# A fused attention, gating and convolution kernel: two more additions in the last head pair, and the last two tiles of w_in loaded and converted through both buffers

## The chip, the cores and the metric

The kernel runs on one core of one Trainium2 chip, in one launch. The metric is the device time of that core in microseconds (us); 553.07 us is the median of three runs of the kernel before (552.95 to 553.29).

## The reference, cut to what matters

Three blocks follow one another. Inputs are float32; batch is 4, the sequence 576 long, 8 heads of 64, model width 512.

```python
# 1. attention, per batch and head, rotary q and k
attn = softmax(scale * q_rot @ k_rot.T); x = attn @ v          # -> [4, 576, 512]
# 2. gated MLP ("the MLP" below)
h = gelu_tanh(x @ w_in); u, v = h[..., :512], h[..., 512:]     # w_in is 512 x 1024
v_n = (v - mean(v)) / sqrt(var(v) + 1e-6) * g_ln
gated = u * (w_sg @ v_n + b_sg); x = x + gated @ w_out
# 3. convolution gate
gate = sigmoid(conv5(x)); out = (gate * (x @ w_val)) @ w_out2
```

## The kernel before, in words

**Attention.** The 32 heads are worked as 16 pairs (`NPAIR`, i = 0 to 15), two heads in the two halves of the 128 partitions. For a pair, `st_unit` makes transposed scores in nine units: keys in four chunks of 128, each in two halves of 288 queries (u = 0 to 7, table `UNITS`), and a unit u = 8 for the remaining 64 keys. ScalarE (ACT) takes the exponential of each unit into a tile `E`. `pv_unit` multiplies with v on TensorE (PE, L686 and L696), and `sum_unit` (L708) forms the softmax denominators, also on PE, by multiplying with ones in full float32 (L720): four matmuls per term, one for each head and query half. To have fewer terms, `add_unit` (L666) first adds units on GpSimd (POOL, the additions at L260) into two tiles `AC`, one per query half. `adds(i)` (L663) says how many additions a pair makes: 4 in pairs 9 to 14, so that chunks 0, 1 and 2 lie in `AC`; 2 in the others, pair 15 among them, where chunk 2 stays a term of its own in `sum_unit`. While pair i runs, VectorE (DVE) finds the row maxima of pair i + 1 (`s_unit`), so pair 15 has no such work beside it.

**w_in.** Weights arrive as raw 64-bit numbers. w_in is cut into eight tiles n = 0 to 7 (rows k = n % 4; tiles 0 to 3 hold columns 512 to 1023 and are used first, tiles 4 to 7 hold columns 0 to 511). For a tile, `wa_load` moves 512 KB by a DMA on SyncE's queue (SP) into a buffer `WR`; `wa_abs` takes the absolute value on ACT (L319) into `WT`; `wa_half`, twice, turns half a tile into float32 by four DVE instructions (L309, L311, L313, L315) into `WF`; `wa_split` copies the high part to `w_h` on ACT (L263) and subtracts it on POOL for the low part `w_l` (L260). There are two sets of the buffers: number 0 lives until the MLP's end, number 1 belongs to attention's memory and is given up with it. `place(n)` (L331) says which a tile uses: even and odd by turns up to tile 5, then buffer 0 for tiles 6 and 7. Tiles 4 and 5 are converted after pair 14, beside the preparation of the MLP's first input (`x_mult`, `x_high`, `x_low` for four head pairs), and tile 6 is loaded then (`job_v`, L435). Tiles 6 and 7 are converted in the MLP's part of the program (L1120 to L1122): tile 7's load waits until tile 6 has left buffer 0.

**The MLP's start.** `part_a(0)` runs three units of x times columns 512 to 1023 (tiles 0 to 3), each followed by a Gelu into a tile `gl` (L894), statistics, a scaling and a split into `vn` or, for the third unit, `t4` (shown as t); then four units `u_unit` with columns 0 to 511 (tiles 4 to 7, in the order of k); then four `g_unit` with `vn` and `t4`. The results `XH`, `XL` of the preparation are read by the first units.

**Memory and order.** The closing of attention's memory (`close_att`, L1095) is a task that depends on every task of attention, and what writes the MLP's tiles depends on it. By the sizes in the order of the code, the first `gl` tile lies at bytes 97,280 to 101,376 from the right edge; attention's `rc` (denominators) lies at 99,920 to 99,992 and its buffer `WR` number 1 at 99,992 to 104,088, so both are under it. A planner (`Plan`) takes tasks with a cost, their dependencies and a due time worked back from the end, and writes out one order per engine. PE keeps the order of the program; the other engines' queues and SP's are sorted by readiness and due time. Tasks marked `lock` on DVE and POOL are planned so as not to run at the same time. After attention there are the MLP for the three other batches, and the last block.

Of the kernel before, what the change touches and what calls it, by code (L numbers as in the profile page):

```python
# [22 lines left out]
NPAIR = B * HP  # L23
FOUR = 9
# [3 lines left out]
class Plan:  # L28
# [6 lines left out]
    def add(self, eng, cost, fn, r=(), w=(), after=(), lat=0.0, lock=False, kb=0.0):  # L35
        k = len(self.tasks)
        deps = set(after)
        for key in r:
            deps.update(self.writer.get(key, ()))
        for key in w:  # L40
            deps.update(self.writer.get(key, ()))
            deps.update(self.readers.get(key, ()))
        for key in r:
            self.readers.setdefault(key, []).append(k)
        for key in w:
            self.writer[key] = [k]
            self.readers[key] = []
        if eng == "PE":
            if self.last_pe is not None:
                deps.add(self.last_pe)  # L50
            self.last_pe = k
        deps.discard(k)
        self.tasks.append((eng, cost, fn, tuple(sorted(deps)), lat, lock, (tuple(w) or tuple(r))[0:1]))
        self.kb.append(kb)
        return k
# [87 lines left out]
def dve(n):  # L143
    return 0.08 + n / 960


def dve2(n):
    return 0.08 + n / 1920


def act(n):
    return 0.11 + 0.833e-3 * n
# [18 lines left out]
def mixer_kernel(ctx: ExitStack, tc: tile.TileContext, qk, v, vrem, cs, w_in, g_ln, w_sgT, b_sg,  # L171
# [4 lines left out]
    P = Plan()  # L176
# [11 lines left out]
    def tiles(pool_, name, n, shape, dt):  # L188
        T[name] = [pool_.tile(shape, dt, name=f"{name}{j}") for j in range(n)]
        return T[name]  # L190
# [23 lines left out]
    w_h = pA.tile([128, 4, 1024], F32R, name="w_h")  # L214
    w_l = pA.tile([128, 4, 1024], F32R, name="w_l")
# [4 lines left out]
    WR = tiles(pA, "wr", 1, [128, 512, 2], I32)  # L220
    WF = tiles(pA, "wf", 1, [128, 512], F32)
    WT = tiles(pA, "wt", 1, [128, 512], F32)
# [33 lines left out]
    def tt(e, out_, a, b, op, n, r, w, after=()):  # L256

        if e == "D":
            return add("DVE", dve(n), lambda: nc.vector.tensor_tensor(out_(), a(), b(), op), r, w, after, lock=True)  # L259
        return add("Pool", pool(n), lambda: nc.gpsimd.tensor_tensor(out_(), a(), b(), op), r, w, after, lock=True)  # L260

    def acopy(out_, in_, n, r, w, after=()):
        return add("Act", act(n), lambda: nc.scalar.copy(out_(), in_()), r, w, after)  # L263

    def pool_waits(src, r):

        return [add("Pool", 0.1, lambda: nc.gpsimd.tensor_copy(mark[0:1], src()), r, [("mark",)])]

    def split(hi, lo, src, n, rk, kh, kl, e="P", after=()):

        acopy(hi, src, n, rk, [kh], after)
        tt(e, lo, src, lambda: hi().bitcast(F32), ALU.subtract, n, [*rk, kh], [kl])
# [26 lines left out]
    def f64_to_32(raw, f, t, keys, n, after=()):  # L299


        kr, kf, kt = keys

        def i32(x):
            return x().bitcast(I32)

        def top():
            return raw()[:, :, 1]
        return [add("DVE", dve2(n), lambda: nc.vector.tensor_scalar(t(), t(), MIN_NORMAL, None, ALU.max), [kt], [(*kt, n, "x")],  # L309
                    after, lock=True),  # L310
                add("DVE", dve2(n), lambda: nc.vector.tensor_scalar(  # L311
                    i32(t), i32(t), 3, 0x3FFFFFF8, ALU.logical_shift_left, ALU.bitwise_and), w=[(*kt, n, "x")], lock=True),
                add("DVE", dve(n), lambda: nc.vector.scalar_tensor_tensor(  # L313
                    i32(t), raw()[:, :, 0], 29, i32(t), ALU.logical_shift_right, ALU.bitwise_or), [kr], [(*kt, n, "x")], lock=True),
                add("DVE", dve(n), lambda: nc.vector.scalar_tensor_tensor(  # L315
                    i32(f), top(), -0x40000000, i32(t), ALU.bitwise_and, ALU.bitwise_or), [kr, (*kt, n, "x")], [kt, kf], lock=True)][-1]

    def f64_abs(raw, t, keys, n, after=()):
        add("Act", act(n), lambda: nc.scalar.activation(t(), raw()[:, :, 1].bitcast(F32), AF.Abs), [keys[0]], [keys[2]], after)  # L319

    def weight_load(y, src, after=()):
        dma(512, lambda q: q.dma_start(out=WR[y].rearrange("p a b -> p (a b)"), in_=src), w=[("wr", y)], after=after)
# [6 lines left out]
        split(dst_h, dst_l, lambda: WF[0], 512, [("wf", 0)], (name, "h"), (name, "l"))  # L329

    def place(n):  # L331
        return n % 2 if n < 6 else 0

    def wa_load(n, after):
        k, hf = n % 4, 1 - n // 4
        weight_load(place(n), w_in[128 * k:128 * k + 128, 1024 * hf:1024 * hf + 1024], after)

    def wa_abs(n, after):
        y = place(n)
        f64_abs(lambda: WR[y], lambda: WT[y], [(m, y) for m in ("wr", "wf", "wt")], 512, after)  # L340

    def wa_half(n, x, after):
        y, cc = place(n), slice(256 * x, 256 * x + 256)
        k = f64_to_32(lambda: WR[y][:, cc], lambda: WF[y][:, cc], lambda: WT[y][:, cc], [(m, y) for m in ("wr", "wf", "wt")], 256, after)
        return [k]

    def wa_split(n, after):
        y, k, hf = place(n), n % 4, 1 - n // 4
        cc = slice(512 * hf, 512 * hf + 512)
        split(lambda: w_h[:, k, cc], lambda: w_l[:, k, cc], lambda: WF[y], 512, [("wf", y)], (f"win{k}_{hf}", "h"), (f"win{k}_{hf}", "l"),  # L350
              after=after)

    def sg_load(k, after):
# [24 lines left out]
    def wa_whole(n, after):  # L378
        wa_abs(n, after)
        for x in range(2):  # L380
            wa_half(n, x, after)
        wa_split(n, after)
# [35 lines left out]
    def job_v(i, after, rot):  # L418

        last = []  # L420
        if i % 2 and i < 8:
            wa_abs(i // 2, after)
        if not i:
            last = pool_waits(lambda: RAW[0][0:1, 1, 0, S - 1:S], [("raw", 0, 1)])
        if 1 <= i < 9:
            y, x = (i - 1) // 2 % 2, (i - 1) % 2
            wa_half((i - 1) // 2, x, rot)
            last = pool_waits(lambda: WF[y][0:1, 256 * x + 255:256 * x + 256], [("wf", y)])
        if i == 9 and FOUR > 9:
            last = pool_waits(lambda: RAW[1][0:1, 1, 0, S - 1:S], [("raw", 1, 1)])  # L430
        if FOUR <= i < NPAIR - 1:
            j3 = (i + 1) % 3
            low_part("D", i + 1, 1, rot)
            last = pool_waits(lambda: KL[j3].bitcast(F32)[0:1, S - 1:S], [("kl", j3)])
        if i == NPAIR - 2:  # L435
            for hp in range(2):
                x_mult(0, hp, after, "D")
                x_high(0, hp, after)
                x_low(0, hp, after)
                x_load(0, hp + 2, after)  # L440
            for n in (4, 5):
                wa_whole(n, after)
            wa_load(6, P.writer["xs", 1])
            for hp in (2, 3):
                x_mult(0, hp, after, "D")
                x_high(0, hp, after)
                x_low(0, hp, after)
        return last


# [110 lines left out]
    def low_part(e, i, j, after):  # L561

        j2, j3 = i % 2, i % 3
        hi, lo, kh, kl = ((QH, QL, "qh", "ql"), (KH, KL, "kh", "kl"))[j]
        tt(e, lambda: lo[j3], lambda: RAW[j2][:, j, 0], lambda: hi[j3].bitcast(F32), ALU.subtract, S,
           [("raw", j2, j), (kh, j3)], [(kl, j3)], after)
        if j:
            dma(32, lambda q: dg(q, KRL[j3], KL[j3]), [("kl", j3)], [("krl", j3)], n=2)
# [92 lines left out]
        EU[i, u] = n  # L661
        add("Act", 0.62, lambda: nc.scalar.activation(E[n], ps[:, :, 0:HALF], AF.Exp), [kps], [("e", n)])  # L662
    def adds(i):  # L663
        return 4 if FOUR <= i < NPAIR - 1 else 2

    def add_unit(i, u):  # L666

# [173 lines left out]
    def x_mult(b, hp, after=(), e="P"):  # L841
        i, y = 4 * b + hp, hp % 2
        tt(e, lambda: XS[y][:, 4:], lambda: XS[y][:, 4:], lambda: RB[y][:, 4:], ALU.mult, S, [("rb", y)], [("xs", y)], after)
        dma(290, lambda q: q.dma_start(out=x_d[i], in_=XS[y][:, 4:]), [("xs", y)], [("x_d", i)])

    def x_high(b, hp, after=()):
        add("Act", act(S), lambda: nc.scalar.copy(XH[:, hp], XS[hp % 2][:, 4:]), [("xs", hp % 2)], [("X", hp, "h")], after)

    def x_low(b, hp, after=()):
        return [tt("D", lambda: XL[:, hp], lambda: XS[hp % 2][:, 4:], lambda: XH[:, hp].bitcast(F32), ALU.subtract, S,  # L850
                   [("xs", hp % 2), ("X", hp, "h")], [("X", hp, "l")], after)]
# [243 lines left out]
    def close_att():  # L1095
# [21 lines left out]
    P.writer.update({k: [opened["1"]] for k in (  # L1117
        [("gl", x) for x in range(2)] + [("gl", x, y) for x in range(2) for y in range(2)] + [("vs", x) for x in range(2)]
        + [("st", x) for x in range(3)] + [("u", x) for x in range(4)] + [("vn", x, m) for x in range(6) for m in "hl"])})
    wa_whole(6, ())  # L1120
    wa_load(7, ())
    wa_whole(7, ())  # L1122
    for b in range(B):
        part_a(b)
        if b == 0:
# [100 lines left out]
```

## Time and profile before

| quantity | value |
|---|---|
| median of three runs | 553.07 us |
| the profiled execution | 553.03 us, of which the traced span is 551.2 us |
| PE busy | 542.0 us, 98% of the span |
| DVE, ACT, POOL busy | 407.1, 276.9, 247.8 us |
| granted TensorE clock | 0.999 of 2.4 GHz |
| DMA | 77.83 MB, 141 GB/s mean |

Start times in a trace are us from the span's start. PE is the matmul row, whose ends are modelled and overlap, so a matmul's own duration is longer than its share of a dense row: the spacing of starts tells what it costs. In a chain or timeline a line gives the start, the duration, the engine and source line, and how many instructions were merged. A bracket tells the idle time of the engine before it and what ended it.

### The profile page before, as it was taken

To read this page: it belongs to the slowest core of one execution; us is meant where nothing else is said; L and a number is where in the kernel's file an instruction comes from. 1 tells how busy PE (TensorE), PEld (TensorE's weight loads), DVE (VectorE), ACT (ScalarE), POOL (GpSimd) and SP (SyncE) were. 2 spreads that over 40 slices of the span, in tenths; PEclk is the share of its full clock that TensorE was granted. 3 is DMA by queue.
4 is the path that set the end of the run, shared out by engine and by line. 5 is a ranking of instruction groups with operands and counts; after the bars stand their busy time and mean duration, and the time that the engine had idled before them with its cause. 6 is when DMAs were issued, how large, how long until landed. Compare 5 with 4: busy or idle time off the path is not lost.

```text
span 551.2 us, 11755 instructions
## 1 busy us (share of the span) xinstructions
PE 542.0 (98%) x4592; PEld 463.8 (84%) x4592; DVE 407.1 (74%) x593; ACT 276.9 (50%) x449; POOL 247.8 (45%) x229
## 2 busy tenths in 40 slices
PE   7999999999999999999999999999999999999996
PEld 5877777777777777679989989989999998899985
DVE  5878888888888888869767556655979997659610
ACT  2566666667666667635426136134157443433321
POOL 4645555454565555458966677554610021222000
PEclk9999999999999999999999999999999999999999
DMA  6565656555666664684583752643263212110022
GB/s 218 142 178 160 181 155 175 160 158 169 186 169 168 173 190 111 183 254 110 156 286 103 227 192 76 194 143 124 104 211 122 76 44 77 39 58 1 0 77 96
DMA packets 58120, 77.83 MB, mean 141 GB/s; under 512 B 29392, under 2 KB 34000, under 8 KB 58064
## 3 DMA queue, kind: packets, MB, share of 16 engines
q1 hardware_dynamic: 57920, 77.08, 46.7%
q8 instruction: 36, 0.59, 0.4%
q14 instruction: 20, 0.16, 0.1%
q10 hardware_dynamic: 144, 0.00, 0.0%
HBM read 56.38 MB, written 18.95 MB: 137 GB/s over the span
## 4 chain that ended last, share of the span: by engine, by line
PE 96%; DVE 2%; DMA 1%; ACT 0%; issue 0%; SPq 0%; ACTq 0%; DVEq 0%
PE ps L827 55%; PE ps L649 12%; PE ps L686 12%; PE ps L720 6%; PE ps L657 4%; PE ps L597 4%; PE ps L696 2%; PE ps L938 2%; DVE raw L259 1%; DVE mx L600 1%; DMA cst<-cs 1%; PE ps L607 1%; DVE mn L609 0%; ACT ob L263 0%; ACT kh L263 0%
## 5 line engine op out<-in xcount | busy, mean ns | idle before, releaser
L600 DVE TENSOR_REDUCE mx<-ps 128x2 f32<-128x640 f32 (+1 forms) x96 | 89.1, 957 | 28.6 <-PE ps L597 21.7
L662 ACT ACTIVATE e<-ps 128x576 f32<-128x576 f32 x144 | 87.1, 652 | 20.0 <-PE ps L657 10.9
L686 PE MATMUL ps<-e,vm 128*64 128x288 f32 x512 | 65.6, 409 | 0.0
L686 PEld LDWEIGHTS ps<-e,vm 128*64 128x64 f32 x512 | 35.3, 137 | 24.7 <-issue 2.6
L260 POOL TENSOR_TENSOR ac<-e,e 128x576 f32<-128x576 f32 x32 | 45.1, 1430 | 9.5 <-ACT e L662 9.5
L827 PE MATMUL ps<-s_h,vn 128*128 128x288 f32 x256 | 46.9, 295 | 0.0
L259 DVE TENSOR_TENSOR raw<-raw,cst 128x1152 f32<-128x1152 f32 (+1 forms) x33 | 41.9, 1271 | 6.3 <-DMA cst<-cs 6.3
L263 ACT CAST qp<-raw 128x512 fp32r<-128x512 f32 x16 | 18.6, 1162 | 48.7 <-DVE raw L259 48.7
L827 PEld LDWEIGHTS ps<-s_h,vn 128*128 128x128 f32 x256 | 38.3, 188 | 0.0
L649 PE MATMUL ps<-qh,kh 64*128 64x288 f32 x256 | 38.3, 295 | 0.0
L649 PE MATMUL ps<-qh,kl 64*128 64x288 f32 x256 | 37.9, 292 | 0.0
L649 PE MATMUL ps<-ql,kh 64*128 64x288 f32 x256 | 37.8, 292 | 0.0
L649 PE MATMUL ps<-mr,one_r 64*128 64x288 f32 x256 | 37.7, 291 | 0.0
L260 POOL TENSOR_TENSOR vs<-vs,u 128x576 f32<-128x576 f32 x16 | 26.9, 1684 | 19.9 <-DVE vs L942 19.8
L597 PE MATMUL ps<-kh,qp 64*128 64x320 f32 (+1 forms) x256 | 32.7, 311 | 1.8 <-ACT kh L263 1.8
L1019 DVE SCALAR_TENSOR_TENSOR gt<-xm,cw,gt 128x576 f32<-128x576 f32 x32 | 29.0, 910 | 1.8 <-ACT gt L1016 1.4
L597 PEld LDWEIGHTS ps<-kh,qp 64*128 64x128 f32 x256 | 21.7, 184 | 9.5 <-ACT kh L263 7.6
L309 DVE TENSOR_SCALAR wt<-wt 128x256 f32<-128x256 f32 (+1 forms) x28 | 16.0, 570 | 16.7 <-ACT wt L319 16.7
L260 POOL TENSOR_TENSOR xl<-xs,xh 128x576 fp32r<-128x576 f32 x2 | 5.3, 2632 | 50.0 <-ACT xh L263 50.0
L827 PE MATMUL ps<-XL,w_h 128*128 128x288 f32 x128 | 27.4, 296 | 0.0
L827 PE MATMUL ps<-XH,w_h 128*128 128x288 f32 x128 | 27.4, 295 | 0.0
L827 PE MATMUL ps<-XH,w_l 128*128 128x288 f32 x128 | 27.4, 295 | 0.0
(178 smaller groups left out, 1489.0 us busy)
## 6 DMA issues: line engine op xcount, KB each, us to landing
raw<-qk SPq DMA_DIRECT2D x31, 576.0 KB
xu_d<-xu SPq DMA_DIRECT2D x32, 144.0 KB
rb<-r_d SPq DMA_DIRECT2D x32, 144.0 KB
xs<-xu_d SPq DMA_DIRECT2D x16, 288.0 KB
x_d<-xs SPq DMA_DIRECT2D x16, 288.0 KB
g_d<-vs SPq DMA_DIRECT2D x16, 288.0 KB
vm<-v SPq DMA_DIRECT2D x16, 256.0 KB
wr<-w_in SPq DMA_DIRECT2D x8, 512.0 KB
```

The lines of the kernel that those rows point to most:

```text
L259: return add("DVE", dve(n), lambda: nc.vector.tensor_tensor(out_(), a(), b(), op), r, w, after, lock=True)
L260: return add("Pool", pool(n), lambda: nc.gpsimd.tensor_tensor(out_(), a(), b(), op), r, w, after, lock=True)
L263: return add("Act", act(n), lambda: nc.scalar.copy(out_(), in_()), r, w, after)
L597: nc.tensor.matmul(ps[:, h, w * y:w * y + w], QP[j2][rows, c], kh[rows, keys], start=True, stop=True)
L600: add("DVE", MAXIMA[n // 2 > 0][1], lambda: nc.vector.tensor_reduce(out=MX[j2][:, n // 2 > 0, :, chunks[0]:chunks[-1] + 1], in_=ps[:, :, 0 ...
L649: nc.tensor.matmul(ps[:, h, 0:HALF], x[rows, keys] if o < 3 else x[rows], y[rows, cols], start=o == 0, stop=o == 3)
L657: nc.tensor.matmul(ps[:, hf, 0:HALF], x, y[:, cols], start=o == 0, stop=o == 3)
L662: add("Act", 0.62, lambda: nc.scalar.activation(E[n], ps[:, :, 0:HALF], AF.Exp), [kps], [("e", n)])
L686: nc.tensor.matmul(pv[64 * hf:64 * hf + 64, h, 0:HALF], VM[j2][:, j, h], E[EU[i, us[hf]]][:, h], start=j == 0, stop=False, skip_group_chec ...
L720: nc.tensor.matmul(ps[32 * t:32 * t + 32, 0, 0:HALF], x[t // 2], a[:, y], start=n == 0, stop=n == len(src) - 1, skip_group_check=True)
L827: nc.tensor.matmul(out_(y), lhs(p, k, y), rhs(q, k, y), start=not z, stop=ends and z == len(terms) - 1)
L1019: add("DVE", dve(S) + 0.05, lambda dd=dd, m=m, x2=x2, gt=gt: nc.vector.scalar_tensor_tensor(gt(), x2()[:, m:m + S], cw[:, 5 * dd + m:5 * d ...
```

## The change

In the last pair, `adds` gives 4 in place of 2: two more POOL additions, and `sum_unit(15)` has one term of four matmuls fewer. Tile 6 of w_in uses raw buffer 1 and tile 7 raw buffer 0 (`place`), both with `WF` and `WT` number 0 (`keys_of`). Tile 7 is loaded when tile 4 has left buffer 0, and is converted whole among attention's tasks; tile 6 is loaded when tile 5 has left buffer 1, and its absolute value and its conversion are among attention's tasks too. In the MLP's part only the split of tile 6 is left, with the subtraction on DVE in place of POOL.

```diff
     def place(n):
-        return n % 2 if n < 6 else 0
+        return n % 2 if n < 6 else 7 - n
+
+    def keys_of(n):
+        return [("wr", place(n)), *[(m, place(n) if n < 6 else 0) for m in ("wf", "wt")]]
...
     def wa_abs(n, after):
-        y = place(n)
-        f64_abs(lambda: WR[y], lambda: WT[y], [(m, y) for m in ("wr", "wf", "wt")], 512, after)
+        keys = keys_of(n)
+        f64_abs(lambda: WR[keys[0][1]], lambda: WT[keys[2][1]], keys, 512, after)
...
-    def wa_split(n, after):
-        y, k, hf = place(n), n % 4, 1 - n // 4
+    def wa_split(n, after, e="P"):
+        y, k, hf = keys_of(n)[1][1], n % 4, 1 - n // 4
...
-            for n in (4, 5):
-                wa_whole(n, after)
-            wa_load(6, P.writer["xs", 1])
+            wa_whole(4, after)
+            wa_load(7, P.writer["xs", 1])
+            wa_whole(5, after)
+            wa_load(6, ())
             for hp in (2, 3):
                 x_mult(0, hp, after, "D")
                 x_high(0, hp, after)
                 x_low(0, hp, after)
+            wa_whole(7, after)
+            wa_abs(6, after)
+            for x in range(2):
+                wa_half(6, x, after)
...
     def adds(i):
-        return 4 if FOUR <= i < NPAIR - 1 else 2
+        return 4 if FOUR <= i else 2
...
-    wa_whole(6, ())
-    wa_load(7, ())
-    wa_whole(7, ())
+    wa_split(6, (), "D")
     for b in range(B):
         part_a(b)
```

(`wa_half` is changed in the same way: raw data from the tile's own `WR`, `WF` and `WT` from `keys_of`.)

## Rows read from the trace of the kernel before

**Rows 1.** The page's chain that ended last, by engine.

```profile
PE 96%; DVE 2%; DMA 1%; ACT 0%; issue 0%; SPq 0%; ACTq 0%; DVEq 0%
```

**Rows 2.** Who waited for whom, engine PE, whole span: total, times, longest.

```profile
PE ps L741 <- POOL mr L294: 2.8, 1, 2.8
PE ps L597 <- ACT kh L263: 1.8, 2, 1.1
```

**Rows 3.** The chain in order of time: start, us, what; attention's end and the MLP.

```profile
222.63 1.59 PE ps L720 x24
...
234.69 2.08 PE ps L720 x32
236.77 29.81 PE ps L827 x180
...
316.74 29.61 PE ps L827 x180
...
396.51 150.15 PE ps L827 x888
```

**Rows 4.** Timeline of PE, 222 to 270 us: first reads of four operands.

```profile
235.61 0.67 PE L720 MATMUL ps<-ac,ones 128*32 128x288 f32 x8
...
241.81 0.61 PE L827 MATMUL ps<-w_h,XL 128*128 128x512 f32 x2
...
252.01 0.43 PE L827 MATMUL ps<-XH,w_h 128*128 128x288 f32 x2
...
266.41 0.29 PE L938 MATMUL ps<-s_h,t 128*128 128x288 f32 x1
```

**Rows 5.** Timeline of POOL, 205 to 270 us.

```profile
216.09 2.80 POOL L260 TENSOR_TENSOR ac<-ac,e 128x576 f32<-128x576 f32 x2
...
226.42 3.09 POOL L260 TENSOR_TENSOR ac<-e,e 128x576 f32<-128x576 f32 x2 [5.24 <-ACT e L662]
229.47 1.33 POOL L260 TENSOR_TENSOR rr<-xr_l,rr 128x512 f32<-128x512 f32 x1
...
234.61 1.80 POOL L260 TENSOR_TENSOR xr_l<-rr,xr_h 128x512 fp32r<-128x512 f32 x1
...
262.29 3.10 POOL L260 TENSOR_TENSOR t<-gl,t 64x512 fp32r<-64x512 f32 x2
```

**Rows 6.** Timeline of DVE, 205 to 270 us.

```profile
225.56 0.30 DVE L311 TENSOR_SCALAR wt<-wt 128x256 int32<-128x256 int32 x1
...
226.69 1.53 DVE L309 TENSOR_SCALAR wt<-wt 128x256 f32<-128x256 f32 x1
228.26 1.40 DVE L311 TENSOR_SCALAR wt<-wt 128x256 int32<-128x256 int32 x1
...
232.77 2.50 DVE L259 TENSOR_TENSOR XL<-xs,XH 128x576 fp32r<-128x576 f32 x2
235.19 1.50 DVE L315 SCALAR_TENSOR_TENSOR wf<-wr,wt 128x256 int32<-128x256 int32 x1
...
239.24 0.42 DVE L315 SCALAR_TENSOR_TENSOR wf<-wr,wt 128x256 int32<-128x256 int32 x1
```

**Rows 7.** Timeline of ACT, 205 to 270 us.

```profile
225.08 4.45 ACT L662 ACTIVATE e<-ps 128x576 f32<-128x576 f32 x8 [0.33 <-PE ps L649]
...
235.81 0.69 ACT L319 ACTIVATE wt<-wr 128x512 f32<-128x512 f32 x1 [1.73 <-DMA wr<-w_in]
...
246.72 1.28 ACT L894 ACT_TABLE_LOAD   x1 [1.49 <-DMA x_d<-xs]
```

**Rows 8.** SP's queue: its timeline, 205 to 270 us.

```profile
230.61 0.60 SPq L322 DMA_DIRECT2D wr<-w_in  x1
...
242.12 0.54 SPq L733 DMA_DIRECT2D r_d<-rc  x1
...
246.45 1.26 SPq L865 DMA_DIRECT2D rr<-r_d  x2
```

**Rows 9.** SP's queue: who waited for whom, 200 to 260 us.

```profile
SPq L865 <- DMA r_d<-rc: 0.5, 1, 0.5
```

More of the change, by code (lines that the diff above doesn't have):

```diff
@@ L338, in wa_abs @@
     def wa_abs(n, after):
-        y = place(n)
-        f64_abs(lambda: WR[y], lambda: WT[y], [(m, y) for m in ("wr", "wf", "wt")], 512, after)
+        keys = keys_of(n)
+        f64_abs(lambda: WR[keys[0][1]], lambda: WT[keys[2][1]], keys, 512, after)
     def wa_half(n, x, after):
-        y, cc = place(n), slice(256 * x, 256 * x + 256)
-        k = f64_to_32(lambda: WR[y][:, cc], lambda: WF[y][:, cc], lambda: WT[y][:, cc], [(m, y) for m in ("wr", "wf", "wt")], 256, after)
+        keys, cc = keys_of(n), slice(256 * x, 256 * x + 256)
+        z, y = keys[0][1], keys[1][1]
+        k = f64_to_32(lambda: WR[z][:, cc], lambda: WF[y][:, cc], lambda: WT[y][:, cc], keys, 256, after)
         return [k]
-    def wa_split(n, after):
-        y, k, hf = place(n), n % 4, 1 - n // 4
+    def wa_split(n, after, e="P"):
+        y, k, hf = keys_of(n)[1][1], n % 4, 1 - n // 4
         cc = slice(512 * hf, 512 * hf + 512)
-        split(lambda: w_h[:, k, cc], lambda: w_l[:, k, cc], lambda: WF[y], 512, [("wf", y)], (f"win{k}_{hf}", "h"), (f"win{k}_{hf}", "l"),
+        split(lambda: w_h[:, k, cc], lambda: w_l[:, k, cc], lambda: WF[y], 512, [("wf", y)], (f"win{k}_{hf}", "h"), (f"win{k}_{hf}", "l"), e,
               after=after)
```

## The prediction

> **What bounds the kernel now.** I read the page's chain first: TensorE (PE) carries 96% of it [rows 1]. Next the waits of PE: in the whole span it waited twice, 2.8 us for the first tile it reads and 1.8 us for `kh`, both in the first 30 us of the start [rows 2]. Then the chain in order of time: from pair 15 on, piece follows piece without a gap. `sum_unit(15)` starts at 234.69 and takes 2.08; the MLP's first matmul is at 236.77, and 234.69 + 2.08 = 236.77. The 180 matmuls of the first batch's MLP up to its first `t4` matmul take 29.81 us, the same 180 of the third batch 29.61, and the last block is one dense piece of 150.15 us [rows 3]. So every microsecond taken from PE's program comes off the end, as long as no engine makes PE wait, and work moved on ACT, DVE, POOL or SP is worth nothing by itself. What it can do is use up slack. The timelines of the other engines are for that: I look there for what each operand's last writer leaves until PE reads it.
>
> **Part one: two additions for four matmuls.** A `sum_unit` with four terms is 32 records and 2.08 us, one with three terms is 24 records and 1.59 us, as in pair 14 just before [rows 3]. PE loses one term: 2.08 - 1.59 = 0.49 us. Nothing lies beside these matmuls on PE, so the whole 0.49 is on the path.
>
> POOL gets two additions more. A pair of them took 2.80 in pair 14, 1.40 each, and 3.09 for the two first ones of pair 15, 1.55 each [rows 5]. The two first end at 226.42 + 3.09 = 229.51. The other two need the fifth and sixth exponential; the eight run from 225.08 for 4.45, 0.56 each, so the sixth is done near 228.4 and does not hold them [rows 7]. Back to back they end at 229.51 + 2.80 = 232.3, or 232.6 at 1.55 each. PE reads `ac` at 235.61 now, and at 235.61 - 0.49 = 235.12 with a term less in front [rows 4]. Slack: 2.5 us or more. The cover is PE's own work on the pair, the products with v; without it the two additions would cost their 2.8 us.
>
> Behind them on POOL stand the product `rr` (1.33, now at 229.47), a `w_l` subtraction and `xr_l` [rows 5]. They move back by up to 2.8 us. `xr_l`, done at 234.61 + 1.80 = 236.41 now, would be done at 239.2; it is read by the MLP's third unit, and at 241.81 PE is still in the first [rows 4], so nobody on PE waits.
>
> What the additions do to DVE has a price. Two `tensor_scalar` of the conversion of tile 5, which take 0.30 when POOL is idle, took 1.53 and 1.40 while POOL added [rows 6, 5]: each ended as an addition did. Two additions more can hold DVE for up to 2 x 1.40 = 2.8 us. DVE's work that PE waits for is `XL`: now done at 232.77 + 2.50 = 235.27 [rows 6], its last pair first read at 241.81 [rows 4]. That is 6.5 us of slack, against 2.8. The Trainium skill ("SBUF — State Buffer", section "Who interferes with whom") says that GpSimd and a VectorE instruction of this kind take one port pair by turns, and that the second to come is blocked for the other's whole instruction. The 1.53 and 1.40 agree with it. By that rule the added work on POOL is DVE time too; it speaks against the change, and the rival on the slow side below is where it would show.
>
> **Part two: tiles 6 and 7.** The same eight DVE instructions per tile, the same absolute values, copies and two loads are issued; only tile 6's subtraction changes engine. Tile 7's load takes the place that tile 6's has now: issued 230.61, landed by 235.81, where ACT takes the absolute value, 5.2 us later [rows 8, 7]. From there the conversion now ends at 239.24 + 0.42 = 239.66 [rows 6], 3.85 us after the landing. Tile 7's split follows; its parts (k = 3) are read after tile 6's (k = 2), so after 252.01 [rows 4]. Cost on PE: nothing, with some twelve microseconds of cover by PE's first units.
>
> Tile 6's load must wait for tile 5 to leave buffer 1. Tile 5's last instruction ends at 235.19 + 1.50 = 236.69 [rows 6]. Load 5.2, absolute value and conversion 3.85: 236.69 + 5.2 + 3.85 = 245.7. Then a copy on ACT and a subtraction on DVE, well under 2 us together by the neighbouring rows of such sizes. PE first reads this tile (k = 2) at 252.01 [rows 4]. Slack about 4 us, and PE's first units are the cover. On SP the load's wait holds up what stands behind it, the last pair's small stores among them, by at most the lateness of tile 5.
>
> The conversion of tile 6 is now something that the MLP's first Gelu waits for: attention's memory closes behind it, and buffer 1 lies under the first `gl`. Today the Gelu's table load starts at 246.72 [rows 7]. The DMA named there is not what it needs; another queue entry, reading the denominators, waited for the store `r_d<-rc` and was issued at 246.45, so that store, issued at 242.12, had landed just then [rows 8, 9], and `rc` lies under `gl`. So the Gelu has to wait till about 246.5 for memory anyway, and 245.7 fits under it. Behind the Gelu the chain through statistics, scaling and split ends in `t4` at 262.29 + 3.10 = 265.39 [rows 5], read at 266.41 [rows 4]: 1.0 us of slack, the smallest I found. It should grow, since tile 7's work leaves the engines of that chain.
>
> **The sum.** -0.49 + 0 + 0. The profiled execution is 553.03 with a span of 551.2; 553.03 - 0.49 = 552.54. The median shown is 0.04 above it: 553.07 - 0.49 = 552.58, about 552.6, or 0.09%. At the most 0.20 more could come off, if the first batch's piece became as dense as the third's (29.81 - 29.61) [rows 3]; at the least nothing, if `ac` comes as late as the term was long. I take 0.49, since the row with three terms is the same operation.
>
> **Rivals.**
>
> *The first Gelu comes late (slower).* Place: tile 5 out of buffer 1, then load, conversion, close of attention's memory, Gelu, `t4`. With the load issued at 236.69 it has 246.72 - 245.7 = 1.0 us, and `t4` 1.0 more. So PE waits from an issue after 238.7, the saving is gone at 239.2, and the loss is over 1.1 us at 240.3. For it: DVE held by the two additions (2.8) brings the issue to 239.5; two more instructions of the conversion held as the one of 235.19 was (1.50 against 0.42) add 2.2, so the equivalent of 241.7, and a PE wait of 3.0: 552.58 + 3.0 = 555.6. Against it: the planner gives what the close waits for an earlier due time, and tile 7 no longer stands in the Gelu's way. With the 2.8 alone, the load issued at 239.5, PE would wait 0.8 and the time be 553.4. That is what the Trainium skill's rule on the port pair, taken in full, would make of the change.
>
> *`ac` comes late.* `rr` and the subtraction of tile 4 stand before the last addition on POOL, each stretched as `xr_l` was (1.80 for 1.33 of such work): 232.6 + 1.8 + 1.8 = 236.2, a wait of 1.1 on PE, 553.7. For it: both are ready near then. Against it: the additions are due first, as PE needs them first.
>
> *The second part does not do what it says.* Tile 6 still turns to float32 near 245, beside the MLP's first unit, not in attention. Likely, and the time is the same 552.6, as nothing on PE waited for tiles 6 and 7 before.
>
> *Faster by more.* Only 0.49 + 0.20 is in sight on PE; 1.1 would need matmuls to run denser than any row shows.
>
> **How the numbers follow.** About 0.2%, 1.1 us, is what a measurement of this kernel can tell from no change. Forecast, PE undisturbed, 552.3 to 552.8, with the rival that tile 6 is not moved in time in it: 0.76. `ac` late: 0.07. The Gelu late by little (552.8 to 554.1): 0.05; late by much: 0.09. Faster by over 1.1 us: 0.03. So faster 0.03, same 0.76 + 0.07 + 0.05 = 0.88, slower 0.09. The range 552.2 to 553.6 holds the forecast and half of the 0.12 that lies between, 0.82; what it leaves out is mostly the late Gelu.
>
> **What would show it.** Right: the last `sum_unit` with 24 records and about 1.6 us, four POOL additions in pair 15 ended before 233, PE's waits still only the two of the start, the MLP's first matmul some 0.5 earlier, the table load on ACT not later than 246.7. Wrong: a PE wait at L720 for `ac`, at L938 or L827 for `t4` or `vn`, or a table load after 248 behind the conversion of tile 6; or a different spacing of matmuls with no wait at all.

## The result: 0.7% slower, with a first Gelu that came 6 us later

The changed kernel takes 556.68 us (median of 4 runs, 556.44 to 557.16) against 553.01 for the kernel before in runs beside it: a ratio of 1.0070, 95% interval 1.0058 to 1.0082. That is 3.7 us slower, where 552.6 was forecast and 553.6 was the top of the range. The profiled execution took 556.59 with a span of 554.8; the granted TensorE clock was 0.999 as before. One execution each of e2 and e3 below took over 763 us at a granted clock of 0.657 and 0.754 and is in none of the medians and ratios here. In the kernel after, the code lies 9 lines lower from `adds` on (L720 is now L729, L827 is L836, L894 is L903, L938 is L947).

Engine shares of the page's chain that ended last, after; PE carried 96% of it before [rows 1]:

```profile
PE 86%; DVE 5%; DMA 2%; POOL 2%; ACT 1%; issue 1%; SPq 0%; DVEq 0%; ACTq 0%; POOLq 0%
```

Ten points more of the chain now run through other engines. Which operand PE stood for is in the view of who waited for whom (total, times, longest), where before only the two waits of the start stood [rows 2]:

```profile
PE ps L947 <- POOL t L260: 1.7, 1, 1.7
...
PE ps L836 <- ACT w_h L263: 1.3, 1, 1.3
PE ps L836 <- ACT gl L903: 0.3, 1, 0.3
```

All three are in the first batch's MLP, as PE's timeline tells:

```profile
234.40 0.69 PE L729 MATMUL ps<-e,ones 128*32 128x288 f32 x8
234.91 0.67 PE L729 MATMUL ps<-ac,ones 128*32 128x288 f32 x8
235.39 0.67 PE L729 MATMUL ps<-e,ones_b 128*32 128x288 f32 x8
235.99 0.73 PE L836 MATMUL ps<-w_h,XH 128*128 128x512 f32 x2
...
252.76 0.53 PE L836 MATMUL ps<-XH,w_h 128*128 128x288 f32 x2 [1.29 <-ACT w_h L263]
...
269.84 0.40 PE L947 MATMUL ps<-s_h,t 128*128 128x288 f32 x1 [1.70 <-POOL t L260]
```

The first four rows are part one as forecast: three groups of eight, `ac` read at 234.91 without a wait, the MLP's first matmul at 235.99. The second batch's first matmul is in PE's timeline at 281.67, at 278.05 before, so the first batch takes 281.67 - 235.99 = 45.68 where it took 278.05 - 236.70 = 41.35 (its first matmul starts at 236.70 in PE's timeline before). **That stage alone loses 4.33 us.** The three waits are 3.3 of it; the rest stands in the matmuls right behind each wait, as in the four that read `t4`: 0.81 in the chain after, 0.53 in the other batches. What follows is unchanged: the third batch's piece is 29.61 and the last block 150.15, as in [rows 3]. Attention, from the first `sum_unit` to the MLP's first matmul, gains 0.47.

Back from the waits: ACT's timeline (238 to 256 us) first, since both `w_h` and the Gelu are there.

```profile
238.83 0.67 ACT L319 ACTIVATE wt<-wr 128x512 f32<-128x512 f32 x1 [3.01 <-DMA wr<-w_in]
...
245.06 0.67 ACT L319 ACTIVATE wt<-wr 128x512 f32<-128x512 f32 x1 [0.72 <-DMA wr<-w_in]
252.09 0.62 ACT L263 CAST w_h<-wf 128x512 fp32r<-128x512 f32 x1 [6.36 <-DVE wf L315]
252.72 1.28 ACT L903 ACT_TABLE_LOAD   x1
```

Tile 7's absolute value is at 238.83, tile 6's at 245.06, and its copy to `w_h` at 252.09, after 6.36 us of idle time in which ACT waited for DVE. The table load of the first Gelu stands right behind that copy: 252.72, where it was 246.72 [rows 7]. So the table load is 6.0 us late. What made tile 6 late stands on SP's queue and on DVE:

```profile
231.09 0.33 SPq L742 DMA_DIRECT2D r_d<-rc  x1
...
233.47 0.45 SPq L322 DMA_DIRECT2D wr<-w_in  x1
...
237.26 1.27 SPq L713 DMA_DIRECT2D xu_d<-xu  x2
238.63 0.54 SPq L322 DMA_DIRECT2D wr<-w_in  x1
239.82 0.59 SPq L736 DMA_DIRECT2D rc<-ss  x1
```

```profile
226.42 1.52 DVE L309 TENSOR_SCALAR wt<-wt 128x256 f32<-128x256 f32 x1
227.98 1.40 DVE L311 TENSOR_SCALAR wt<-wt 128x256 int32<-128x256 int32 x1
229.41 1.53 DVE L313 SCALAR_TENSOR_TENSOR wt<-wr,wt 128x256 int32<-128x256 int32 x1
230.86 0.27 DVE L741 RECIPROCAL rc<-rc 128x9 f32<-128x9 f32 x2
...
236.93 0.41 DVE L315 SCALAR_TENSOR_TENSOR wf<-wr,wt 128x256 int32<-128x256 int32 x1
...
245.76 1.35 DVE L309 TENSOR_SCALAR wt<-wt 128x256 f32<-128x256 f32 x1 [0.26 <-ACT wt L319]
...
247.47 1.54 DVE L313 SCALAR_TENSOR_TENSOR wt<-wr,wt 128x256 int32<-128x256 int32 x1
249.12 1.48 DVE L315 SCALAR_TENSOR_TENSOR wf<-wr,wt 128x256 int32<-128x256 int32 x1
...
251.63 0.42 DVE L315 SCALAR_TENSOR_TENSOR wf<-wr,wt 128x256 int32<-128x256 int32 x1
```

and beside them on POOL:

```profile
226.20 3.02 POOL L260 TENSOR_TENSOR ac<-e,e 128x576 f32<-128x576 f32 x2 [5.90 <-ACT e L671]
229.19 3.02 POOL L260 TENSOR_TENSOR ac<-ac,e 128x576 f32<-128x576 f32 x2
...
244.42 2.54 POOL L260 TENSOR_TENSOR w_l<-wf,w_h 128x512 fp32r<-128x512 f32 x2 [2.13 <-ACT w_h L263]
247.17 3.14 POOL L260 TENSOR_TENSOR xs<-xs,rb 128x576 f32<-128x576 f32 x2 [0.21 <-DMA xs<-xu_d]
```

Read across: three DVE instructions of tile 5 (226.42 to 230.94) stand beside the additions. Behind them stand two reciprocals, behind these on SP the store `r_d<-rc`, and behind that tile 7's load, issued at 233.47 instead of 230.61 [rows 8]. It isn't the two new additions that delay this load but the new order of the tasks: with the additions alone (e1 below) the first of the two reciprocals comes ahead of these instructions, as in the kernel before, and the load goes out at 230.09; without the additions (e2) it comes behind three held instructions again, and the load goes out at 232.95. SP of e1, then DVE of before, e1 and e2:

```profile
230.09 0.60 SPq L322 DMA_DIRECT2D wr<-w_in  x1
...
225.17 0.21 DVE L732 RECIPROCAL rc<-rc 128x9 f32<-128x9 f32 x1
...
225.49 0.21 DVE L732 RECIPROCAL rc<-rc 128x9 f32<-128x9 f32 x1
...
229.63 1.39 DVE L313 SCALAR_TENSOR_TENSOR wt<-wr,wt 128x256 int32<-128x256 int32 x1
230.94 0.20 DVE L741 RECIPROCAL rc<-rc 128x9 f32<-128x9 f32 x1
```

Tile 5's last instruction ends at 237.34; SP is then in two stores, so tile 6's load goes out at 238.63. It lands by 245.06. Tile 7, whose `WF` and `WT` tile 6 takes over, is converted only at 243.68 (ACT copies it at 243.72). The conversion of tile 6 meets POOL's subtractions `w_l` and products `xs`: of its eight instructions one took 1.35 instead of 0.29 and two took 1.54 and 1.48 instead of 0.43, and it ends at 252.05.

### The profile page after: what moved, and what is told of

Read it like the earlier page. It is cut to its first block, busy times and chain, and to the rows that moved or that the text cites. A ratio compares the mean times of both kernels' runs of the same rounds, so it can differ in the third digit from the quotient of the medians.

```text
span 554.8 us, 11744 instructions
## 1 busy us (share of the span) xinstructions
PE 542.7 (98%) x4584; PEld 464.0 (84%) x4584; DVE 422.3 (76%) x594; ACT 276.9 (50%) x449; POOL 247.6 (45%) x230
## 4 chain that ended last, share of the span: by engine, by line
PE 86%; DVE 5%; DMA 2%; POOL 2%; ACT 1%; issue 1%; SPq 0%; DVEq 0%; ACTq 0%; POOLq 0%
PE ps L836 49%; PE ps L658 11%; PE ps L695 10%; PE ps L729 5%; PE ps L606 3%; PE ps L666 3%; PE ps L705 2%; PE ps L947 2%; DMA rc<-ss 1%; DVE xs L259 1%; DMA x_d<-xs 1%; PE ps L616 1%; POOL vn L260 1%; DVE wt L313 1%; DVE wf L315 1%
## 5 line engine op out<-in xcount | busy, mean ns | idle before, releaser
L836 PE MATMUL ps<-s_h,vn 128*128 128x288 f32 x256 | 46.9, 295 | 0.0
L836 PEld LDWEIGHTS ps<-s_h,vn 128*128 128x128 f32 x256 | 38.4, 188 | 0.0
L836 PE MATMUL ps<-XH,w_h 128*128 128x288 f32 x128 | 27.6, 297 | 1.6 <-ACT w_h L263 1.3
L836 PE MATMUL ps<-XH,w_l 128*128 128x288 f32 x128 | 27.5, 296 | 0.0
L836 PE MATMUL ps<-XL,w_h 128*128 128x288 f32 x128 | 27.4, 296 | 0.0
L836 PE MATMUL ps<-s_l,vn 128*128 128x288 f32 x128 | 27.3, 295 | 0.0
```

The source lines that it names most:

```text
L836: nc.tensor.matmul(out_(y), lhs(p, k, y), rhs(q, k, y), start=not z, stop=ends and z == len(terms) - 1)
```

## The experiments

The expectations name their theories by letters. Theory A is the main one: tile 6, loaded and converted ahead of the Gelu, makes the Gelu late; POOL's products beside its conversion are part of that (A1). Rivals: the two additions do it by themselves (B); tile 7 in attention does it (D); or a late Gelu costs nothing and PE's loss comes from elsewhere. The table gives three stages of each profiled kernel, from PE's and ACT's timelines: attention (first `sum_unit` to the MLP's first matmul), the first batch (to the second batch's first matmul), and the start of the first Gelu's table load. Each ratio is to executions of the kernel before made beside that kernel (medians 552.78 to 553.09), so ratios compare better than medians.

| kernel | attention, us | first batch, us | table load at | median, us | ratio to before (95%) |
|---|---|---|---|---|---|
| before | 205.57 | 41.35 | 246.72 | 553.01 | |
| after | 205.10 | 45.68 | 252.72 | 556.68 | 1.0070 (1.0058 to 1.0082) |
| e1 additions only | 205.09 | 41.80 | 247.32 | 553.49 | 1.0008 (0.9999 to 1.0017) |
| e2 weights only | 205.57 | 44.43 | 252.42 | 555.87 | 1.0051 (1.0033 to 1.0070) |
| e3 Gelu held | 205.60 | 43.47 | 251.12 | 554.93 | 1.0037 (1.0025 to 1.0049) |
| e4 POOL held, addresses moved | 205.11 | 43.45 | 250.69 | 557.10 | 1.0076 (1.0062 to 1.0090) |
| e5 POOL held | 205.19 | 43.62 | 250.91 | 554.48 | 1.0021 (1.0010 to 1.0032) |
| e6 tile 6 in MLP | 204.97 | 42.05 | 245.52 | 553.86 | 1.0016 (1.0006 to 1.0025) |
| e8 `rc` elsewhere | 204.99 | 42.07 | 247.03 | 553.12 | 1.0006 (0.9994 to 1.0017) |
| e9 one task later | 205.06 | 42.02 | 247.25 | 553.16 | 1.0003 (0.9994 to 1.0012) |
| e10 two tasks later | 205.05 | 41.98 | 247.40 | 553.29 | 1.0002 (0.9994 to 1.0011) |
| e11 and `w_l` on DVE | 205.07 | 41.38 | 246.42 | 552.76 | 0.9997 (0.9988 to 1.0006) |

In single executions the first `sum_unit` starts anywhere from 30.89 to 31.48, so a stage's length says more than its clock time.

**The two parts alone.** e1 is the kernel before with part one, e2 the kernel after without it:

```diff
 # e1, against the kernel before
-        return 4 if FOUR <= i < NPAIR - 1 else 2
+        return 4 if FOUR <= i else 2
 # e2, against the kernel after: the same line back
```

> Only the two more additions in pair 15; w_in as before. Theory A (the loss comes from tile 6 of w_in standing in front of the first Gelu): TensorE loses one term of sum_unit and waits for nothing new, 0.49 us less, about 552.5; the table load ahead of the first Gelu stays within 1 us of 246.7. Theory B (the two additions hold VectorE, and through it SyncE's queue, and that alone delays the chain): the table load 3 us late or more, and a time of 554 or more.

> Only the change of w_in's last two tiles; pair 15 keeps two additions. Theory A: the first Gelu still stands behind tile 6's conversion and its copy on ScalarE; TensorE waits for the copy and for t4 as in the changed kernel, 3 to 4 us, so 556 to 557. Theory B: without the additions VectorE and the load are on time, the conversion ends near 245.7, and the time is that of the kernel before, 553.0 to 553.3. Between the two (554 to 555): both parts are needed for the whole loss.

Part two alone brings 2.8 us of the loss (0.0051 of 553), part one alone at most 0.9, with a table load only 0.6 late: rival B is out, and so is the gain that Theory A expected of e1 (about 552.5). In e2 both loads go out back to back at 232.95, tile 6's some 5 us earlier than in the kernel after, yet the table load is at 252.42, 0.3 earlier. So an earlier load of tile 6 buys little by itself. ACT's timeline of e2 names another last releaser than in the kernel after:

```profile
239.66 0.67 ACT L319 ACTIVATE wt<-wr 128x512 f32<-128x512 f32 x1 [3.54 <-DMA wr<-w_in]
240.23 0.40 ACT L733 ACTIVATE ss<-ps 128x288 f32<-128x288 f32 x1
243.46 0.62 ACT L263 CAST w_h<-wf 128x512 fp32r<-128x512 f32 x1 [2.83 <-DVE wf L315]
243.98 0.66 ACT L319 ACTIVATE wt<-wr 128x512 f32<-128x512 f32 x1
250.63 0.62 ACT L263 CAST w_h<-wf 128x512 fp32r<-128x512 f32 x1 [5.99 <-DVE wf L315]
252.42 1.28 ACT L903 ACT_TABLE_LOAD   x1 [1.18 <-DMA r_d<-rc]
```

Tile 6's absolute value (243.98) stands behind tile 7's whole conversion and copy, not behind a load: both tiles use `WT` and `WF` number 0 (`keys_of`). The copy of the denominators `ss` stands on ACT behind tile 7's absolute value, which waited for its load; the last reciprocal (250.52) then stands on DVE behind tile 6's whole conversion, and the store of the denominators, which the close of attention waits for too, is last. So tile 6 delays the Gelu in two ways, by its own copy and by the denominators behind its conversion.

e1 keeps all of the 0.48 in attention (205.57 - 205.09) and gives 0.45 back in the first batch. ACT and the chain say where:

```profile
247.32 1.28 ACT L894 ACT_TABLE_LOAD   x1 [1.52 <-DMA rr<-r_d]
...
256.10 0.66 ACT L319 ACTIVATE wt<-wr 128x512 f32<-128x512 f32 x1 [3.46 <-DMA wr<-w_out]
256.67 1.65 ACT L263 CAST vn<-gl 128x512 fp32r<-128x512 f32 x3
```

```profile
266.47 0.80 PE ps L938 x4
```

The absolute value of w_out's first tile was planned ahead of the `vn` copies, and ACT waited 3.46 us for that load. `t4` is then so late that the four matmuls which read it take 0.80 instead of 0.53.

**A late Gelu alone.** e3 is the kernel before with the first Gelu put behind tile 7's copy, a read that orders it and nothing else:

```diff
-                GL()[gi][:, 0:n2], ps[:, 0:n2], AF.Gelu_apprx_tanh), [kp], [kg])
+                GL()[gi][:, 0:n2], ps[:, 0:n2], AF.Gelu_apprx_tanh), [kp, *[("win3_0", "h")][:b == c0 == 0]], [kg])
```

> The kernel before, with one dependency more: the first Gelu comes behind the copy of tile 7's high part on ScalarE, which ended at 250.15. Nothing else is changed and all is computed. Theory A: a late Gelu is by itself the loss; it starts its table load at 250.2 in place of 246.7, 3.4 us late; t4 had 1.0 us to spare, so TensorE waits about 2.4 us at the first use of t4, 555.4. Theory B or any other cause (a late load, busy transfers): the chain catches up, under 553.5.

A table load 4.40 late (251.12) lengthens the first batch by 2.12, about half: the chain from the Gelu to `t4` makes up for the rest. That a late Gelu costs nothing is out: 4.4 late cost 0.4% here.

**POOL beside the conversion.** In e4 and e5, the kernel after, POOL's first two `xs` products for the second batch wait until tile 6 is converted, by a one-element copy on POOL that reads the converted tile. They differ in where that copy writes: e4 has a new four-byte tile, cut from a padding tile, and by it `w_h` and every tile behind it on that side lie 32 bytes further on in the built program (`w_h` at 47,616 instead of 47,584); e5 writes into a padding tile that was there, and no tile moves.

```diff
+            if b == 1 and not hp:
+                hold = [add("Pool", 0.1, lambda: nc.gpsimd.tensor_copy(held[0:1, 0:1], WF[0][0:1, 511:512]), [("wf", 0)], [("held",)])]
+            x_mult(b, hp, hold if b == 1 else ())
```

> The changed kernel with GpSimd held back by one tiny copy that reads the last element of tile 6's float32 form, so that its two products for the next batch run after the conversion, not beside it. Theory A1 (the conversion took 7.0 us and not 3.85 because three of its instructions stood behind GpSimd's, 1.35, 1.54 and 1.48 us in place of 0.29, 0.43 and 0.42): the conversion ends 3.2 us earlier, near 248.9, the table load starts near 249.5, the wait for tile 6's copy on TensorE goes and that for t4 falls below 1 us; 553.3 to 554. Theory A2 (the late load is what counts, VectorE would have waited anyway): the end moves by less than 1 us, 555.7 or more.

> The run before it once more (the changed kernel, GpSimd's two products for the next batch held until tile 6 is converted), with the tiny copy writing into a tile that is there already, so that no address moves. In that run the second batch's MLP began at 279.74 against 281.83 of the changed kernel, but its matmuls ran slower from there (27.18 for 26.89, 151.31 for 150.15). Theory A1: with the addresses kept the matmuls are those of the changed kernel, the second batch begins about 2 us earlier than its 281.8 and the time is about 554.5. Theory C (the held products cost elsewhere what they give here): 556.5 or more again, with the slower matmuls.

e4 was to be faster and was the slowest of all: 557.10, ratio 1.0076 (1.0062 to 1.0090). Its second batch begins 2.1 us earlier than in the kernel after, but everything behind is slower. Lines of its chain, against 26.89 and 150.15 in the kernel after:

```profile
279.74 27.18 PE ps L837 x168
...
399.20 151.31 PE ps L837 x888
```

In e5 these pieces are 26.89 and 150.15 again, and the time is 554.48: 2.2 us below the kernel after. Its POOL timeline:

```profile
250.31 0.17 POOL L866 COPY pad<-wf 1x1 f32<-1x1 f32 x1 [2.65 <-DVE wf L315]
250.44 3.29 POOL L260 TENSOR_TENSOR xs<-xs,rb 128x576 f32<-128x576 f32 x2
```

With the products moved to 250.44, tile 6's conversion takes 5.36 from its absolute value to its end (244.88 to 250.24) instead of 6.99, and the table load is 1.81 earlier. A1 holds, for about 2 us of the 3.7. POOL's subtractions `w_l`, which weren't moved, still hold two instructions of that conversion (0.93 and 1.27 instead of 0.29 each); the 4.2 us that the table load is still late are those, the two tiles' later loads and tile 7's conversion in front.

**Tile 6 out of attention.** e6 is the kernel after, with the additions and with tile 7 among attention's tasks, but tile 6 in buffer 0 again, loaded and converted in the MLP's part:

```diff
-        return n % 2 if n < 6 else 7 - n
+        return n % 2 if n < 6 else 0
...
-            wa_load(6, ())
...
-            wa_abs(6, after)
-            for x in range(2):
-                wa_half(6, x, after)
...
+    wa_load(6, ())
+    wa_abs(6, ())
+    for x in range(2):
+        wa_half(6, x, ())
     wa_split(6, (), "D")
```

> The changed kernel with tile 6 alone undone: it is loaded into buffer 0 behind tile 7 and converted in the MLP's part, still split with VectorE; tile 7 stays among attention's tasks, the additions stay. Theory A (tile 6 in front of the first Gelu is the loss): the table load is back within 1.5 us of 246.7, 552.5 to 554. Theory D (tile 7 among attention's tasks is enough, as ScalarE waits for its load ahead of the denominators): the table load after 249 and 555 or more.

The table load is at 245.52, earlier than in the kernel before, the waits for `t4` and the Gelu are gone, and 2.8 us of the loss with them. **With e1, this decides between A and the rivals**: tile 7 in attention (D) and the additions (B) are both still in this kernel. The 0.16% that remain go to PE's one wait in the MLP, 0.3 us for tile 6's `w_l`, and to something that this profile, the fastest of its ten runs, doesn't show.

**What the first Gelu waits for.** The prediction said that the Gelu had to wait for the store of `rc` because `rc` lies under `gl`. e8 is e1 with `rc` at the end of attention's memory and a filler of its size in its old place (attention's other tiles move too, by 128 bytes):

```diff
-    RC = tiles(att, "rc", 2, [128, 9], F32)
+    for j in range(2):
+        att.tile([128, 9], F32, name=f"padrc{j}")
...
+    RC = tiles(att, "rc", 2, [128, 9], F32)
```

> The kernel before with the two additions, and the small tile of the denominators moved to the end of attention's memory, a filler of its size left in its place; nothing else changes its address but the tile itself. Theory A: the first Gelu waits for the store of the denominators because that tile lies under the first gl; without it the table load follows the absolute value of tile 7 at about 245.3 in place of 247.3 in the run with the additions alone, t4 is ready some 1 to 2 us earlier, TensorE waits for nothing, and the 0.49 us of the shorter sum_unit show: 552.3 to 552.6. Rival (the wait is for all of attention's memory at once, wherever a tile lies): table load and time as in that run, 552.6 to 553.5.

```profile
247.03 1.28 ACT L896 ACT_TABLE_LOAD   x1 [1.11 <-DMA rr<-r_d]
```

The table load still waits, till 247.03. The built programs say why: in the kernel before, the first `gl` tile takes bytes 148,448 to 152,544 of a partition, while `rc` lies at 219,584 and `WR` number 1 at 219,712. So neither was ever under it, and the sizes taken "in the order of the code" ahead of the prediction misled. The first Gelu there, in the kernel after and in e8 stands behind semaphores of PE, POOL and six or seven DMA queues, one of them for the last store `r_d<-rc`: the close of attention's memory makes it wait for the last users of that memory, wherever a tile lies. Tile 6 counts in the same way, since `WR` number 1 belongs to that memory.

**Can the 0.49 us be kept?** e9 is e1 with the absolute value of w_out's first tile put behind the third Gelu; e10 also puts the small conversion of `cw` behind `t4`; e11 is e9 with tile 7's subtraction on DVE:

```diff
 # e9
-        f64_abs(lambda: WR[0], lambda: WT[0], keys, 512)
+        f64_abs(lambda: WR[0], lambda: WT[0], keys, 512, third if name == "wo0" else ())
 # e11, besides
-        wa_split(n, after)
+        wa_split(n, after, "D" if n == 7 else "P")
```

> The two additions alone, with the absolute value of w_out's first tile planned behind the third Gelu of the first batch. In the run with the additions alone that instruction stood ahead of the copies of vn on ScalarE and waited there 3.46 us for its load, and the chain to t4 was some 3 us later than in the kernel before, its table load only 0.6. Theory E (the 0.49 us of the shorter sum_unit are given back in the first batch, because the chain to t4 lost its slack to that wait): t4's first half is done before 265.5, TensorE needs 41.4 to 41.5 from the MLP's first matmul to the second batch, and the time is 552.3 to 552.7. Rival F (the chain loses to the additions themselves, by instructions of VectorE that stand behind GpSimd's): t4 near 266.4 again, 41.8 or more, 552.8 to 553.5.

> The same with, besides, the conversion of the small convolution weights (20 columns, four instructions of VectorE) planned behind the first batch's t4; in the run with the additions alone it took 1.28, 1.22, 1.21 and 0.18 us between 241.2 and 245.2 as GpSimd was busy. Theory E: nothing more to gain on TensorE, 552.3 to 552.7. Theory F: VectorE is free some 2 us earlier ahead of tile 7's conversion, t4 comes earlier than in the run beside it, and this one alone gains.

> The kernel before with the two additions, the absolute value of w_out's first tile behind the third Gelu, and tile 7's subtraction on DVE in place of POOL. If what gave the 0.49 us back in the last runs was tile 7's low part, late on POOL behind the two xs products, then PE waits for no operand after attention (the 0.4 for w_l is gone), the piece from the MLP's first matmul to the second batch's first is about 41.4 to 41.6 as in the kernel before (42.0 without this edit), and the time is 552.3 to 552.7, ratio about 0.999. If the term was never worth 0.49, or another operand is late next (vn, t), the piece stays at 41.8 or more and the time at 553.0 to 553.4.

e9 and e10 missed. In figures it is rival F of e9's text that came: the first half of `t4` is done at 266.42 (264.70 + 1.72), where e1 has 266.41, the first batch takes 42.02, and instructions of tile 7's conversion stand behind POOL's `xs` products (1.41 and 1.55 on DVE). PE, however, waits for another operand ahead of `t4`: tile 7's `w_l`, which comes behind that conversion. PE's waits and POOL's timeline of e9:

```profile
PE ps L827 <- POOL w_l L260: 0.4, 1, 0.4
```

```profile
246.17 2.99 POOL L260 TENSOR_TENSOR xs<-xs,rb 128x576 f32<-128x576 f32 x2 [1.50 <-DMA xs<-xu_d]
252.15 1.28 POOL L260 TENSOR_TENSOR w_l<-wf,w_h 128x512 fp32r<-128x512 f32 x1 [3.00 <-ACT w_h L263]
```

With the subtraction on DVE, e11 has no PE wait after the start. Its chain:

```profile
236.24 29.82 PE ps L827 x180
...
277.70 26.89 PE ps L827 x168
```

From 236.24 to 277.70 are 41.46 us; before, 236.77 to 278.21 were 41.44. So the 0.50 gained in attention isn't given back in this execution. It took 552.40 against 553.03. The median, 552.76 beside 553.09, is just above the 552.3 to 552.7 that were expected; the interval of the ratio holds 1, so e11 isn't clearly faster than the kernel before, and no version tried is.

## Why the prediction was wrong, and where it was right

**Right: what part one does by itself.** One term of 0.49 left PE, the four additions ended at 232.21 (232.3 was said), PE didn't wait for `ac`, and `XL`, done at 237.00, was in time. **Right in mechanism: the rival "the first Gelu comes late (slower)"**, with its place, its chain and PE waits at L938 and L827. It had chances of 0.05 (late by little) and 0.09 (by much) and prices of 553.4 to 555.6; the run gave 556.7. It charged PE one for one for what was late beyond the slack, where e3 lost 2.12 for 4.40; its place was right, but it had the delay in the issue of the load, and most of it came behind that.

**Wrong: "Load 5.2, absolute value and conversion 3.85: 236.69 + 5.2 + 3.85 = 245.7 ... and 245.7 fits under it."** Each term was a duration from a place where little lay beside it, and each grew:

| term | forecast | kernel after |
|---|---|---|
| tile 7 converted, ahead of tile 6 | 239.66 | 243.68: its load went out at 233.47, not at 230.61 |
| load issued | 236.69 | 238.63: tile 5 ended 0.65 later, and SP was in two stores for 1.27 |
| load | 5.2 | 6.4 (238.63 to 245.06); tile 7's, landed by 238.83, was no longer beside it; by then `WT` was free only since 243.68 |
| absolute value and conversion | 3.85 | 7.0 (245.06 to 252.05), beside POOL |
| tile 6's copy on ACT, ahead of the Gelu | not in the sum | 0.62 |
| table load | 246.5 or earlier | 252.72 |

The biggest miss is the conversion, 3.1 us. e5 shows that about half of it (1.63) is POOL's `xs` products; most of the rest stands beside POOL's `w_l`. The prediction had the rows for this (0.30 became 1.53 beside an addition, [rows 5, 6]) and applied them to part one, not to the conversion that part two moves into a stretch where POOL also works; the rival's price took two held instructions there, and three were held. The Trainium skill ("SBUF — State Buffer", section "Who interferes with whom") has the second of the two engines blocked for the other's whole instruction; the trace agrees, with 1.48 against 0.43 for the same operation. That tile 6 shares `WT` and `WF` with tile 7 had no term in the sum.

**Wrong: "Slack about 4 us" for tile 6 at 252.01.** The same sum stood under it. Tile 6 was converted at 252.05 instead of 245.7, and PE waited 1.29 for its copy, on its own, before any Gelu was late for PE.

**Wrong: "`rc` lies under `gl`"** and "buffer 1 lies under the first `gl`" as reasons for the Gelu's wait (e8 and the built addresses). The wait was there, for the close of attention's memory as a whole, so this failed step moved no number of the sum.

**Wrong: "the whole 0.49 is on the path"**, for part one alone. It is on PE's path, but the operands behind it had less slack than the forecast gave them: `t4` 1.0 on paper and, with the additions in, less than nothing (e1), also when w_out's absolute value was out of its way (e9, 266.42 again), and there tile 7's `w_l` was late too. Only e11 keeps it.

The loss of 3.7 us: tile 6 in front of the Gelu is 2.8 of it (e6 against after), POOL's products beside its conversion are about 2 of these (e5), and a late Gelu alone costs about half of its lateness (e3). Open: the 0.16% left in e6, and why tile 6's load took 6.4 us instead of 5.2; e2, with that load 5 us earlier and the Gelu as late, suggests that it matters little.

## What to carry to other kernels

Before a task is put in front of a barrier, add up the whole chain to the barrier with the durations that its steps have in company: the issue behind what its queue already holds, the load beside the other transfers of its stretch, the task in front that holds the same buffers, and each VectorE instruction as long as the GpSimd instruction next to it. A margin of 1.0 us is none where one held instruction costs 1.1 more. And half a microsecond taken from the engine that bounds is kept only if every operand read behind it has that much slack; look for the next late one, and move that.

## What the runs showed of the hardware

- A 128x20 instruction of DVE takes 0.16 to 0.18 us with POOL idle (243.61 in the kernel after) and took 1.21 to 1.36 beside POOL's subtractions and products (242.38 in e6, 241.16 in e1), about what one of 128x256 took there: its size hardly mattered. Not each one was held: in the kernel before, one at 241.52 took 0.20 while POOL worked from 240.40 to 242.94.
- A small transfer can land late. The denominators (`rc<-ss`), issued on SP at 239.82 behind tile 6's load, reached the reciprocal after 5.4 us, as the chain of the kernel after has it; before, issued at 239.06 (SP's timeline), they were there for the reciprocal at 241.39 (DVE's). That the load ahead is the reason isn't shown: in e8 those of pair 14, issued at 227.24 ahead of the load, were there at 231.85.

```profile
239.82 5.44 DMA rc<-ss
```

- Thirty-two bytes can cost 0.8 to 1.1% of a dense stretch. e4 and e5 are the same instructions in the same order and differ in where the tiles lie; e4's last block of 888 matmuls took 151.31 instead of 150.15, the 168 matmuls of a batch 27.18 instead of 26.89. The granted clocks, 0.998 and 1.0, differ by less. Which of the moved tiles it is wasn't tried.
